# Kernelized attention and two expert layers on one core: the attention's TensorE work of a pair issued as one chunk

## The chip, the cores and the metric

The kernel runs on one core of one Trainium2 chip. The metric is the device time of one execution in microseconds; the kernel before takes 1374.68 us (median of three runs, 1373.49 to 1375.31).

## The reference

Three layers follow one another. Only the first is touched by the change.

```
proj = x @ w_phi                      # 64 -> 128 features, for q and for k, per head
proj = proj - max(abs(proj))          # over the 128 features of a token
phi  = concat(exp(proj), exp(-proj))  # 256 features
kv   = k_p.T @ v;  z = sum(k_p)       # over the 576 tokens
out  = (q_p @ kv) / (q_p . z + 1e-6)
# then x @ w_in, ELU, @ w_out         # 2304 x 512 -> 2048 -> 512
# then 4 experts: relu(x @ w1[e]) @ w2[e], weighted by normalized probabilities
```

There are 4 batches of 8 heads with 576 tokens and 64 channels; two heads make a pair, so there are 16 pairs, four to a batch.

## The kernel before

Attention goes pair by pair. The generator `attention()` (line 340 on) is a three-deep pipeline. In round `i` it holds the new pair `new` (number `i`), the pair `a` (`i-1`) and the pair `z` (`i-2`). Of `new` it makes the projections: `mid()` for the tokens left over from whole blocks of 128 (L229), `keys()` and `queries()` (both L237). After each projection VectorE applies the guard (L211 a maximum, L212 a subtraction), and ScalarE the exponentials of the keys (L215, L216). Of `a` it makes `kv()` (L266, L267; the PSUM bank is copied to `kvw` at L270), the transposes of the guarded queries `qd` (L277, L281, followed by exponentials into `ew`, L286), the denominators `den()` (L295) and the numerators `num()` (L308). `den()` also sends the denominators through a DMA (`dn<-dd`, L299), which lays them out on 128 partitions. Of `z` it makes three steps that need no TensorE: `rec()` (L314, L315 on VectorE, then the DMA L316 to DRAM), `spread()` (two DMAs L321, which read the reciprocals back over all partitions into `rb`), and `put_x()` (L327 on VectorE, then the two halves `xh` and `xl` of the attention's output on ScalarE, L333, and GpSimd, L336).

```
def rec(self):
    with tc.issue_after(mark[0]):
        V.tensor_scalar(out=dn, in0=dn, scalar1=1e-6, ...)
        V.reciprocal(out=dn, in_=dn)
    SP.dma_start(rscr[self.i]..., dn)
def spread(self):
    for h in range(2):
        SP.dma_start(self.rb[h * D:h * D + D], rscr[self.i]...)
def put_x(self):
    with tc.issue_after(mark[0]):
        V.tensor_tensor(out=xf, in0=xf, in1=self.rb, op=ALU.mult)
```

`mark[0]` is the last guard or Elu instruction issued on VectorE, so `rec()` and `put_x()` come behind it there. `dn`, `dd` and `rb` have one buffer each, `nd` has two. A `yield True` ends a chunk, a `yield False` does not.

The first four pairs are run ahead of everything else (the prologue). Then the second layer, `Elu`, begins. It is cut into 36 units, each of 24 matmuls in `l1` (L545 to L547) and 24 in `l2` (L575 to L577), with four calls of `slot()`. Each call adds `rate[0]` to a quota and, for each whole one, runs the attention to its next `yield True`. `RHEAD` is the rate for the first two token tiles, `RATE` for the next four. A limit (`limit[0]`) holds the attention at most one batch ahead of the need. Elu's matmuls are ordered behind the attention's last matmul (`pmark`). Its first tile needs `xh` and `xl` of the pairs 0 to 3, one pair for each quarter of its contraction (`kc`). PSUM has seven banks in this part of the kernel for `bank()`; Elu's accumulators take two and its current product one. Weight conversions (L119 to L155) run beside all this on ScalarE, VectorE and GpSimd. The scheduler may change the order of instructions of one engine that do not depend on each other. From about 430 us on there is no attention and no Elu, only the two expert layers (L673 to L777).

## Time and profile before

| | |
|---|---|
| median of three runs | 1374.68 us |
| profiled execution | 1376.91 us, of it span 1374.9 us |
| TensorE busy | 1344.1 us, 98% of the span |
| VectorE, ScalarE, GpSimd busy | 656.0, 594.4, 352.3 us |

TensorE is busy for nearly all of the span. The span lacks some 2 us of the execution's own time, which lie before its first and after its last instruction. L12 means line 12 of the kernel before; a matmul on 32-bit data appears as two instructions, so L237, 16 matmuls for a pair, shows as x32.

### The profile page before, as it was taken

The page shows a single profiled execution, that of the slowest core. Times are in us where ns is not written, and L with a number is a line of the kernel's source. Part 1 is how long each engine was busy: PE and PEld are TensorE (multiplying, and loading weights), DVE is VectorE, ACT ScalarE, POOL GpSimd, SP SyncE. Part 2 cuts the span into 40 slices and gives each one's busy share as a digit, 9 for nine tenths or more (in the row PEclk, how much of TensorE's full clock was granted, in tenths as well). Part 3 has the DMA queues.
Part 4 walks back from the last instruction along what each step waited for, and adds up shares of the span by engine and source line. Part 5 has one row for each costly group of instructions (what it writes and reads, how often), then busy time and mean ns, then how long its engine had stood idle before and what let it go on. Part 6 is the DMA issues. An engine that isn't in the chain of part 4 may idle for free.

```text
span 1374.9 us, 21612 instructions
## 1 busy us (share of the span) xinstructions
PE 1344.1 (98%) x8408; PEld 1220.7 (89%) x8408; DVE 656.0 (48%) x1085; ACT 594.4 (43%) x1268; POOL 352.3 (26%) x353
## 2 busy tenths in 40 slices
PE   8889999999999999989999999999999999999998
PEld 6688989898998999989888888889898988889897
DVE  5687556664754756674342433333432333423232
ACT  5687555555566554654333351213331213422121
POOL 2478333223463111264110350001420003500000
PEclk9999999999999999999999999999999999999999
DMA  7733344434423313364322045261354341542511
GB/s 226 220 90 98 110 122 151 119 123 124 132 85 108 104 47 115 108 240 170 145 103 116 31 161 182 81 212 46 106 193 161 102 151 32 161 161 92 196 58 62
DMA packets 98422, 173.43 MB, mean 126 GB/s; under 512 B 32272, under 2 KB 45712, under 8 KB 98320
## 3 DMA queue, kind: packets, MB, share of 16 engines
q1 hardware_dynamic: 83392, 148.25, 32.7%
q10 hardware_dynamic: 14928, 23.80, 5.5%
q8 instruction: 66, 1.08, 0.3%
q14 instruction: 36, 0.29, 0.1%
HBM read 118.13 MB, written 53.81 MB: 125 GB/s over the span
## 4 chain that ended last, share of the span: by engine, by line
PE 65%; DMA 4%; DVE 3%; issue 2%; ACT 2%; POOL 1%; SPq 0%; ACTq 0%; DVEq 0%; POOLq 0%
PE bank L673 10%; PE bank L675 9%; PE bank L674 9%; PE bank L775 9%; PE bank L776 9%; PE bank L777 9%; PE bank L754 2%; PE bank L753 2%; PE bank L752 2%; DMA yscr<-y 1%; DMA y<-yscr 1%; PE bank L576 0%; DVE y L785 0%; PE bank L577 0%; PE bank L575 0%
## 5 line engine op out<-in xcount | busy, mean ns | idle before, releaser
L673 PE MATMUL bank<-xv,w 128*128 128x384 f32 x840 | 280.1, 337 | 4.5 <-DVE h L690 1.7
L674 PE MATMUL bank<-xv,w 128*128 128x384 f32 x840 | 281.6, 335 | 0.0
L675 PE MATMUL bank<-xv,w 128*128 128x384 f32 x840 | 278.7, 336 | 0.0
L775 PE MATMUL bank<-w,h 128*128 128x512 f32 x576 | 225.7, 398 | 2.0 <-ACT h L689 1.8
L776 PE MATMUL bank<-w,h 128*128 128x512 f32 x576 | 227.3, 395 | 0.0
L777 PE MATMUL bank<-w,h 128*128 128x512 f32 x576 | 203.8, 396 | 0.0
L502 POOL TENSOR_TENSOR w<-wst,w 128x256 fp32r<-128x256 f32 x100 | 79.8, 815 | 412.8 <-ACT w L501 412.7
L673 PEld LDWEIGHTS bank<-xv,w 128*128 128x128 f32 x840 | 157.8, 188 | 14.2 <-DVE h L690 2.0
L674 PEld LDWEIGHTS bank<-xv,w 128*128 128x128 f32 x840 | 157.7, 188 | 5.3
L675 PEld LDWEIGHTS bank<-xv,w 128*128 128x128 f32 x840 | 157.4, 188 | 0.1
L689 ACT ACTIVATE h<-bank 128x384 fp32r<-128x384 f32 x144 | 67.8, 489 | 179.3 <-PE bank L675 105.0
L690 DVE SCALAR_TENSOR_TENSOR h<-bank,h 128x384 fp32r<-128x384 f32 x144 | 78.1, 555 | 138.2 <-ACT h L689 137.9
L775 PEld LDWEIGHTS bank<-w,h 128*128 128x128 f32 x576 | 107.7, 188 | 26.4 <-ACT h L689 4.0
L776 PEld LDWEIGHTS bank<-w,h 128*128 128x128 f32 x576 | 108.2, 188 | 22.8
L777 PEld LDWEIGHTS bank<-w,h 128*128 128x128 f32 x576 | 107.5, 188 | 22.0 <-DVE h L690 0.3
L679 ACT ACTIVATE cmab<-bank 128x384 f32<-128x384 f32 x60 | 29.4, 490 | 191.4 <-PE bank L675 191.4
L687 DVE TENSOR_TENSOR c<-cmab,bank 128x384 f32<-128x384 f32 x48 | 26.6, 554 | 133.1 <-ACT cmab L679 133.1
L545 PE MATMUL bank<-xh,w 128*128 128x256 f32 x288 | 82.7, 287 | 2.7 <-DVE kp L212 2.6
L624 POOL TENSOR_TENSOR xv<-xs,xv 128x768 fp32r<-128x768 f32 x24 | 46.6, 1944 | 147.1 <-ACT xv L623 141.6
L575 PE MATMUL bank<-gh,w 128*128 128x256 f32 x288 | 81.9, 285 | 0.0
L576 PE MATMUL bank<-gl,w 128*128 128x256 f32 x288 | 80.5, 280 | 0.3 <-DVE gl L558 0.3
L546 PE MATMUL bank<-xl,w 128*128 128x256 f32 x288 | 80.5, 280 | 0.2 <-POOL xl L336 0.2
(118 smaller groups left out, 2527.9 us busy)
## 6 DMA issues: line engine op xcount, KB each, us to landing
xv<-xvd SPq DMA_DIRECT2D x42, 768.0 KB, 4.6
wst<-in_w SPq DMA_DIRECT2D x64, 256.0 KB, 2.7
xvd<-xv SPq DMA_DIRECT2D x21, 768.0 KB, 5.3
yscr<-y SPq DMA_DIRECT2D x54, 256.0 KB, 3.7
y<-yscr ACTq DMA_DIRECT2D x54, 256.0 KB, 3.6
kq<-in_kq SPq DMA_DIRECT2D x16, 320.0 KB, 3.0
rb<-rec SPq DMA_DIRECT2D x32, 144.0 KB, 3.2
xscr<-nd ACTq DMA_DIRECT2D x16, 288.0 KB, 3.3
```

The lines of the kernel that those rows point to most:

```text
L502: on[WL[v % len(WL)]].tensor_tensor(out=lo, in0=x, in1=f32(hi), op=ALU.subtract)
L545: PE.matmul(ph[:, j], w[:, 0, c], xh[:, kc], start=(kc == j == 0), stop=False)
L546: PE.matmul(ph[:, j], w[:, 0, c], xl[:, kc], start=False, stop=False)
L575: PE.matmul(o, w[:, 0, c], self.gh[:, j], start=start, stop=False)
L576: PE.matmul(o, w[:, 0, c], self.gl[:, j], start=False, stop=False)
L673: PE.matmul(o, hi[:, c], x[:, 0, kc], start=not more and kc == 0, stop=False, skip_group_check=more)
L674: PE.matmul(o, hi[:, c], x[:, 1, kc], start=False, stop=False, skip_group_check=more)
L675: PE.matmul(o, lo[:, c], x[:, 0, kc], start=False, stop=kc == 1, skip_group_check=more)
L690: mark[0] = V.scalar_tensor_tensor(out=h[:, 1], in0=c, scalar=0.0, in1=f32(h[:, 0]), op0=ALU.max, op1=ALU.subtract).ins
L775: PE.matmul(self.acc, h[:, 0, c], w[:, 0], start=f == 0, stop=False)
L776: PE.matmul(self.acc, h[:, 0, c], w[:, 1], start=False, stop=False)
L777: PE.matmul(self.acc, h[:, 1, c], w[:, 0], start=False, stop=f == 2 * NQ - 1)
```

## The change

In each round the keys and queries of the new pair follow its middle projection at once, and no chunk ends between them. The steps of the pair `z` come after, each as a chunk of its own: reciprocals, spreading, and `put_x()`, which ends a chunk only where no pair `a` remains. There are three chunks to a round before and after. The two rates are raised by a third.

```
--- before.py
+++ after.py
@@ -42,8 +42,8 @@
 LAG = 2
 RING = 16
 PRE = 0.7
-RATE = 0.375
-RHEAD = 0.525
+RATE = 0.5
+RHEAD = 0.7
 WRATE = 3
 WHEAD = 3
 CVB = 3
@@ -345,9 +345,6 @@
             if a:
                 a.kv(0)
                 yield False
-            if z:
-                z.rec()
-            if a:
                 a.tpose(0)
                 a.kv(1)
                 yield False
@@ -355,27 +352,25 @@
                 a.tpose(2)
             if new:
                 new.mid()
-            if a or new:
-                yield True
-            if z:
-                z.spread()
-                yield True
-            if new:
                 keys = new.keys()
                 next(keys)
                 yield False
                 next(keys, None)
                 yield False
-            if z:
-                z.put_x()
-                done[0] += 1
-                yield not new
-            if new:
                 qs = new.queries()
                 next(qs)
                 yield False
                 next(qs, None)
+            if a or new:
                 yield True
+            if z:
+                z.rec()
+                yield True
+                z.spread()
+                yield True
+                z.put_x()
+                done[0] += 1
+                yield not a
             if a:
                 a.den()
                 yield False
```

The order on VectorE in the prologue, while pair 2 (its keys are `kp_478` here) is guarded; `dn`, `nd` and `rb` belong to pair 0, `raw`, `pcs` and `top` to the conversions. Before:

```order
L314 TENSOR_SCALAR dn<-dn 128x9
L124 TENSOR_SCALAR pcs<-pcs 128x512
L315 RECIPROCAL dn<-dn 128x9
L211 TENSOR_REDUCE mx<-bank 128x2
L212 TENSOR_TENSOR md<-bank,mx 128x256
L127 SCALAR_TENSOR_TENSOR top<-raw,pcs 128x512
L211 TENSOR_REDUCE mx<-bank 128x4
L128 TENSOR_SCALAR raw<-top 128x512
L211 TENSOR_REDUCE mx<-bank 128x4
L212 TENSOR_TENSOR kp_478<-bank,mx 128x4x128
L212 TENSOR_TENSOR kp_479<-bank,mx 128x4x128
L327 TENSOR_TENSOR nd<-nd,rb 128x576
```

The same place on VectorE after the change, from the guards of pair 2's queries (`qd_487`, `qd_488`) on:

```order
L212 TENSOR_TENSOR qd_487<-bank,mx 128x512
L212 TENSOR_TENSOR qd_488<-bank,mx 128x512
L127 SCALAR_TENSOR_TENSOR top<-raw,pcs 128x512
L314 TENSOR_SCALAR dn<-dn 128x9
L128 TENSOR_SCALAR raw<-top 128x512
L315 RECIPROCAL dn<-dn 128x9
L123 TENSOR_SCALAR pcs<-pcs 128x512
L124 TENSOR_SCALAR pcs<-pcs 128x512
L211 TENSOR_REDUCE mx<-bank 128x2
L212 TENSOR_TENSOR md<-bank,mx 128x256
L211 TENSOR_REDUCE mx<-bank 128x4
L327 TENSOR_TENSOR nd<-nd,rb 128x576
```

The reciprocal has moved from ahead of pair 2's guards to behind them, and the product with `rb` from ahead of pair 2's queries to the next pair's keys.

The second place is VectorE where Elu begins: before, from the reciprocal of pair 2 over the guards of pair 4 (`kp_795`):

```order
L314 TENSOR_SCALAR dn<-dn 128x9
L315 RECIPROCAL dn<-dn 128x9
L211 TENSOR_REDUCE mx<-bank 128x2
L212 TENSOR_TENSOR md<-bank,mx 128x256
L211 TENSOR_REDUCE mx<-bank 128x4 x2
L212 TENSOR_TENSOR kp_795<-bank,mx 128x4x128
L123 TENSOR_SCALAR pcs<-pcs 128x512
L212 TENSOR_TENSOR kp_796<-bank,mx 128x4x128
L327 TENSOR_TENSOR nd<-nd,rb 128x576
```

After the change, from the last guard of pair 4 (`qd_809`) to the first of pair 5 (`md`), with pair 2's reciprocal and product:

```order
L212 TENSOR_TENSOR qd_809<-bank,mx 128x512
L314 TENSOR_SCALAR dn<-dn 128x9
L123 TENSOR_SCALAR pcs<-pcs 128x512
L315 RECIPROCAL dn<-dn 128x9
L124 TENSOR_SCALAR pcs<-pcs 128x512
L127 SCALAR_TENSOR_TENSOR top<-raw,pcs 128x512
L128 TENSOR_SCALAR raw<-top 128x512
L327 TENSOR_TENSOR nd<-nd,rb 128x576
L211 TENSOR_REDUCE mx<-bank 128x2
L212 TENSOR_TENSOR md<-bank,mx 128x256
```

Between reciprocal and product stand pair 4's guards before, and only conversions after; the guards of pair 5 stand behind the product. The same order repeats for pair 3 behind pair 5's guards.

The third place is TensorE in the Elu stage, behind a pair's last transposes (`md`). Before:

```order
L281 MATMUL bank<-ident,md 128x128 x2
L229 MATMUL bank<-wbd,kq 128x256
L575 MATMUL bank<-gh,w 128x256
L576 MATMUL bank<-gl,w 128x256
L545 MATMUL bank<-xh,w 128x256
```

After, with Elu's lines five numbers lower:

```order
L281 MATMUL bank<-ident,md 128x128 x2
L229 MATMUL bank<-wbd,kq 128x256
L237 MATMUL bank<-wbd,kq 128x128 x16
L570 MATMUL bank<-gh,w 128x256
L571 MATMUL bank<-gl,w 128x256
```

The sixteen projections of keys and queries now follow the middle projection directly; before, Elu's matmuls stood in between. From the last attention matmul to the kernel's end the order on TensorE (5411 matmuls) is the same in both.

## Rows read from the trace of the kernel before

**Rows 1.** Stages: length, busy us of PE, PEld, DVE, ACT, POOL, granted clock, DMA.

```profile
20.00:73.00 53.00, 45.19 (x440) 35.85 (x440) 37.55 (x72) 36.63 (x84) 21.02 (x23) 1.00 0.65 199
...
73.00:125.00 52.00, 48.29 (x455) 43.32 (x456) 43.83 (x72) 41.92 (x90) 42.61 (x39) 1.00 0.26 77
...
125.00:325.00 200.00, 199.87 (x1841) 180.20 (x1841) 118.12 (x204) 120.99 (x262) 66.94 (x68) 1.00 0.42 127
...
325.00:450.00 125.00, 121.75 (x934) 118.31 (x933) 73.62 (x104) 73.10 (x148) 54.75 (x53) 1.00 0.36 111
...
1371.00:1375.00 4.00, 0.00 (x0) 0.00 (x0) 0.75 (x1) 0.00 (x0) 0.00 (x0) 0.70 0.35 131
```

**Rows 2.** TensorE's waits from 0 to 125 us: total, times, longest.

```profile
PE bank L277 <- DVE qd L212: 6.1, 3, 2.6
...
PE bank L545 <- DVE kp L212: 2.6, 1, 2.6
...
PE bank L308 <- DVE qd L212: 1.2, 1, 1.2
```

**Rows 3.** TensorE in order of time (start, length): one period without a wait.

```profile
17.73 0.60 PE L229 MATMUL bank<-wbd,kq 128*128 128x256 f32 x2
...
18.26 2.06 PE L237 MATMUL bank<-wbd,kq 64*128 64x128 f32 x32
...
20.24 1.18 PE L295 MATMUL bank<-ew,kvw 128*32 128x288 f32 x16
...
21.35 2.16 PE L308 MATMUL bank<-ew,kvw 128*64 128x288 f32 x16
...
23.44 1.16 PE L266 MATMUL bank<-vt,kp 128*128 128x128 f32 x8
...
29.10 0.60 PE L229 MATMUL bank<-wbd,kq 128*128 128x256 f32 x2
```

**Rows 4.** TensorE in order of time: the later periods up to Elu's first matmuls.

```profile
57.99 0.60 PE L229 MATMUL bank<-wbd,kq 128*128 128x256 f32 x2
...
69.90 0.30 PE L277 MATMUL bank<-ident,qd 128*128 128x128 f32 x1 [2.64 <-DVE qd L212]
...
72.36 0.60 PE L229 MATMUL bank<-wbd,kq 128*128 128x256 f32 x2
...
81.98 1.10 PE L266 MATMUL bank<-vt,kp 128*128 128x128 f32 x8
```

**Rows 5.** VectorE in order of time: undisturbed guards, then the fourth period's waits.

```profile
19.45 1.29 DVE L211 TENSOR_REDUCE mx<-bank 128x4 f32<-128x512 f32 x2
...
60.12 0.17 DVE L314 TENSOR_SCALAR dn<-dn 128x9 f32<-128x9 f32 x1 [3.08 <-DMA dn<-dd]
...
66.59 0.76 DVE L327 TENSOR_TENSOR nd<-nd,rb 128x576 f32<-128x576 f32 x1 [2.26 <-DMA rb<-rec]
```

**Rows 6.** SyncE's queue in order of time, the fourth period.

```profile
60.57 0.34 SPq L316 DMA_DIRECT2D rec<-dn  x1
...
62.74 1.10 SPq L321 DMA_DIRECT2D rb<-rec  x2
```

**Rows 7.** ScalarE's queue and ScalarE in order of time, around Elu's start.

```profile
53.53 0.55 ACTq L299 DMA_DIRECT2D dn<-dd  x1
...
79.11 0.42 ACT L333 ACTIVATE xh<-nd 128x256 fp32r<-128x256 f32 x1 [0.18 <-DVE nd L327]
```

**Rows 8.** ScalarE in order of time: one pair in the Elu stage.

```profile
294.70 0.60 ACT L270 ACTIVATE kvw<-bank 128x512 f32<-128x512 f32 x1 [1.15 <-PE bank L267]
...
295.19 1.42 ACT L286 ACTIVATE ew<-bank 128x512 f32<-128x512 f32 x4
```

**Rows 9.** TensorE in order of time: the same pair's projections.

```profile
295.16 0.60 PE L229 MATMUL bank<-wbd,kq 128*128 128x256 f32 x2
...
302.75 2.06 PE L237 MATMUL bank<-wbd,kq 64*128 64x128 f32 x32
```

**Rows 10.** TensorE in order of time: the first pair's projections.

```profile
5.53 3.79 PE L237 MATMUL bank<-wbd,kq 64*128 64x128 f32 x32
```

More of the change, by code (lines that the diff above doesn't have):

```diff
@@ L44 @@
 PRE = 0.7
-RATE = 0.375
-RHEAD = 0.525
+RATE = 0.5
+RHEAD = 0.7
 WRATE = 3
@@ L347, in attention @@
                 yield False
-            if z:
-                z.rec()
-            if a:
                 a.tpose(0)
@@ L357, in attention @@
                 new.mid()
-            if a or new:
-                yield True
-            if z:
-                z.spread()
-                yield True
-            if new:
                 keys = new.keys()
@@ L368, in attention @@
                 yield False
-            if z:
-                z.put_x()
-                done[0] += 1
-                yield not new
-            if new:
                 qs = new.queries()
@@ L377, in attention @@
                 next(qs, None)
+            if a or new:
                 yield True
+            if z:
+                z.rec()
+                yield True
+                z.spread()
+                yield True
+                z.put_x()
+                done[0] += 1
+                yield not a
             if a:
```

## The prediction

> **What bounds the kernel now.** I read the stages first, then TensorE's waits, then each engine in order of time. The stages show TensorE busy in 199.87 of 200 us between 125 and 325 us [rows 1]. There it is the bound, and a change of order gives nothing back. It is short of work earlier: 45.19 of 53 us in the prologue (20 to 73 us) and 48.29 of 52 us where Elu begins (73 to 125 us). The list of waits names the cause [rows 2]: transposes (L277) waited 6.1 us for guarded queries `qd`, and two waits behind Elu's start took 2.6 and 1.2 us. All end with VectorE, but VectorE is not full in the prologue (37.55 of 53 us).
>
> Why it is late stands on VectorE itself [rows 5]. In the fourth period `rec()` (L314) stood 3.08 us until the denominators' DMA had landed, and `put_x()` (L327) stood 2.26 us until `rb` had. Both are ahead of the new pair's guards in that engine's queue, so two DMA waits of an old pair hold up the new one. The DMA in question was issued by ScalarE's queue at 53.53 and ended the wait at 60.12, 6.6 us [rows 5, 7]; from the issue of the reciprocals (60.57) to `rb` (66.59) are 6.0 us, of them 2.2 until the second step's issue (62.74) [rows 5, 6].
>
> A period without such waits is the second: from L229 at 17.73 to L229 at 29.10, 11.37 us [rows 3]. The next three periods end at 72.36 [rows 4].
>
> **The change part by part.** No matmul, guard or transfer is added or removed, and TensorE's order behind the attention is the same, so whatever TensorE gains or loses before some 325 us passes to the end.
>
> *Prologue.* Three periods take 72.36 - 29.10 = 43.26 us; without waits 3 x 11.37 = 34.11. So 9.15 us can be had. In the new order the reciprocal comes behind the pair's own guards. Four guards with 512 elements cost eight operations of 0.6 us (two reductions in 1.29 us, pipelined [rows 5]), 4.8 us. The first starts 19.45 - 17.73 = 1.7 us into the period, so the queries are guarded after 6.5 us, with two conversion operations of the same kind after 7.7. The transposes are wanted 23.44 - 17.73 = 5.7 us plus the first half of `kv()` (some 2.3 of the 5.66 us up to 29.10), 8.0 us into it [rows 3]. That fits. By then the denominators have had more than 6.6 us. The product with `rb` now stands among the next pair's keys guards; `rb` lands 6.0 us after the reciprocal, some 3 us into the next period, which costs VectorE 1 to 2 us where its margin is 0.3. I leave 0.7 us of waiting over the three periods: **-8.4 us** (bounds -9.15 and -6).
>
> *Where Elu begins.* Here the change adds a wait. Take 0 at the start of pair 5's middle projection. Pair 2's reciprocal follows pair 4's guards and is ready about 2.4 us before 0 (the 7.7 us above, `put_x()` of pair 1 with its wait, and the reciprocal among conversions make 9.2 of 11.6 us). `rb` lands 6.0 us later, at 3.6. Until then VectorE stands at `put_x()`, and pair 5's guards are queued behind it. Product 0.7, the middle guard 0.8, eight guards and two conversions 6.0: the queries are guarded at 11.1, pair 3's reciprocal is ready at 12.0, its `rb` lands at 18.0. Then the product (0.7), `xh` on ScalarE (0.42 [rows 7]) and `xl` on GpSimd (about as long as the product, 0.7) follow, 19.8, and Elu's six matmuls on pair 3, which end at 20.5. TensorE reaches this point earlier: in the kernel before, the projections of pair 5, Elu's first unit and the sums of pair 4 took 81.98 - 72.36 = 9.62 us [rows 4]. To these come sums and transposes of pair 5 (29.10 - 23.44 = 5.66 [rows 3]) and half of pair 6's projections (1.5), less three matmuls, 16.4 us. So 20.5 - 16.4: **+4.1 us**, bounds 1.3 (`rb` a microsecond faster twice, and no wait at the first) and 6.2.
>
> The granted clock is 1.00 in every stage with matmuls, waits of 2.64 us included, and 0.70 in 1371 to 1375 us, where none runs [rows 1, 4]. [...]
>
> *The two later waits.* The 2.6 and 1.2 us behind Elu's start [rows 2] came from bringing a pair's keys and queries late, right ahead of work that wants their banks. Now 24 to 48 Elu matmuls follow the queries and give the guards time. But conversions still fill VectorE there (43.83 of 52 us [rows 1]). I take 3.8 away and put 1.5 back: **-2.3 us** (bounds -3.8 and +1.2).
>
> *Ten bursts.* For the pairs 6 to 15 all of a pair's projections follow its transposes without Elu between. Seven banks, less three for Elu, leave four, so the third and fourth projection bank are those that ScalarE must first empty. In a pair before, it copied `kvw` at 294.70 and ended the last exponentials at 295.19 + 1.42 = 296.61, 1.45 us after L229 began at 295.16 [rows 8, 9]. The projections came only at 302.75, so this cost nothing. In the new order the third bank is wanted after 0.53 + 0.99 = 1.5 us (L229, then half of L237's 1.98 [rows 3]) and the fourth after 2.0. That is just in time if ScalarE does nothing else first, and one conversion between (0.6) costs up to half a microsecond. From below the cost is 0, from above 1.2 us for each burst (two operations of 0.6); I take 0.2, nearer to the row, where the end was in time: **+2 us** (bounds 0 and 12).
>
> The higher rates move work within the stage: twelve pairs need 36 chunks either way, and the limit holds them back. VectorE has room after 125 us (118.12 of 200). Nothing, then.
>
> The sum: -8.4 + 4.1 - 2.3 + 2.0 = -4.6 us. It is made against the profiled execution (span 1374.9 in 1376.91 us), which is 2.2 us above the median; the difference is taken from the median: 1374.68 - 4.6 = 1370.1 us.
>
> **The rivals.**
> 1. *Elu's start takes the gain back.* The wait for pair 3's `xh` is at its upper end (6.2) and the two later waits come again elsewhere (0 instead of -2.3): -8.4 + 6.2 + 0 + 2.0 = -0.2, 1374.5 us. For it: VectorE and GpSimd are nearly full from 73 to 125 us. Against it: pair 5's work covers a part.
> 2. *Slower: the burst runs out of banks.* ScalarE is behind by two operations at each of ten bursts, 1.2 us each: -8.4 + 4.1 - 2.3 + 12 = +5.4, 1380.1 us. It outweighs the gain from 0.66 us for each burst on. For it: ScalarE has a queue in order, and `xh`, which waits for `rb`, now stands ahead of the burst. Against it: the row in which the exponentials end just in time, and ScalarE's 120.99 busy of 200 us.
> 3. *The clock falls in the new wait.* The first block of L237 in the kernel, when TensorE had just begun, took 3.79 us, the second 2.06 [rows 3, 10]. One such block more (+1.7) and half as much again behind it give +2.6: -2.0, 1372.7 us. The row's granted clock reads 1.00 at the start too, so the price is uncertain.
> 4. *All waits go.* The entry costs its lower bound and the bursts nothing: -8.4 + 1.3 - 2.3 = -9.4, 1365.3 us.
> That the change does little is excluded for the prologue: TensorE's order hardly moves there, but VectorE's does, and that is the engine waited for.
>
> **How the numbers follow.** Forecast 0.47, rival 1 0.20, rival 2 0.12, rival 3 0.08, rival 4 0.13. Less than 0.2% (2.75 us) can't be told from no change in this kernel. Faster: forecast, rival 4 and the better part of a quarter of rival 3, 0.62. Same: rival 1 and most of rival 3, 0.26. Slower: 0.12. The range 1365.8 to 1376.5 leaves out most of rival 2 and the best of rival 4. The forecast's own range is 1368 to 1372.
>
> **What would show it.** In the changed profile the starts of L229 in the prologue should be 11.4 to 12 us apart, pair 5's at about 64 us instead of 72.36. L314 should wait for no DMA in the prologue, and L327 for 3 to 5 us ahead of pair 5's guards. TensorE should show one wait of 3 to 5 us for `xh` or `xl` at some 80 us, and from 125 us on less than 4 us without work. I am wrong if L277 still waits for `qd` for microseconds, if the wait at Elu's start is above 6 us, or if waits at the projections (L237) for ScalarE recur with every pair.

## The result: 20 us slower, and the profile after

The changed kernel takes 1394.78 us (median of 4 runs, 1393.25 to 1397.62), the kernel before 1374.99 us (4 runs, 1373.49 to 1376.38) beside it on the same chip. The ratio is 1.0144, its 95% interval 1.0132 to 1.0157. The forecast was 1370.1 us, the range 1365.8 to 1376.5: wrong in sign.

To see where the time went I give each point of Elu a *loss*: its time less the undisturbed time of all TensorE work that is ordered ahead of it (0.53 us for a pair's L229, 1.98 for its L237 and so on, 11.3 us a pair, close to the 11.37 us period of [rows 3]; 0.118 us for each Elu matmul, as their starts lie apart in the trace). Two kernels that do the same work in another order can be compared by their losses, not by their times. u0, u6, u24 and u35 are the starts of the numbered Elu units, the end of Elu is the first L668 (L673 before), the rest is from there to the end of the span.

```
us lost             to u0   u0-u6   u6-u24   u24-u35   u35-end   sum at end of Elu   rest of span
before              19.4     5.4      3.3       1.4       0.0          29.4             961.5
changed             19.4     8.6      6.7       6.9       4.1          45.6             962.8
```

Five places, then: the prologue gained nothing, Elu's first units lost 3.2 us more than before, the middle 3.4, Elu's last units 5.5, the step to the expert layers 4.1, and the expert layers 1.3. They add to the 17.5 us between the spans 1374.9 and 1392.4; the medians lie 19.8 us apart, since the profiled execution of the kernel before was one of its slower ones.

Lines below 340 have the same number in both kernels, later ones are 5 lower in the changed kernel. The stages of the changed kernel answer to [rows 1] (length, busy us of PE, PEld, DVE, ACT, POOL, granted clock, DMA):

```profile
20.00:73.00 53.00, 48.03 (x416) 37.85 (x412) 34.98 (x63) 35.57 (x80) 20.01 (x20) 0.94 0.61 191
73.00:125.00 52.00, 50.80 (x467) 42.88 (x467) 43.57 (x73) 40.68 (x92) 32.59 (x33) 1.00 0.30 88
125.00:325.00 200.00, 198.38 (x1781) 178.82 (x1781) 113.36 (x200) 122.61 (x256) 73.20 (x75) 1.00 0.38 117
325.00:450.00 125.00, 114.13 (x889) 111.83 (x886) 66.65 (x91) 63.30 (x127) 50.49 (x49) 0.97 0.35 110
```

TensorE is busier in the prologue than before (48.03 against 45.19 us), at a granted clock of 0.94: busy, but partly at half speed (0.50 from 55 to 60 us). From 325 to 450 us it is busy for 7.6 us less. In the kernel before the granted clock is 1.00 throughout, up to the last matmuls.

**The prologue.** Pair 3's L229 in the kernel before:

```profile
42.95 0.60 PE L229 MATMUL bank<-wbd,kq 128*128 128x256 f32 x2
```

TensorE in order of time in the changed kernel (start, length, in brackets the idle time before and what ended it) answers to [rows 4]:

```profile
38.73 0.60 PE L229 MATMUL bank<-wbd,kq 128*128 128x256 f32 x2
...
55.15 0.80 PE L266 MATMUL bank<-vt,kp 128*128 128x128 f32 x2 [4.06 <-ACT kp L216]
59.36 1.06 PE L229 MATMUL bank<-wbd,kq 128*128 128x256 f32 x2
72.47 0.60 PE L229 MATMUL bank<-wbd,kq 128*128 128x256 f32 x2
```

Pair 3's L229 came at 38.73, 4.2 us ahead of the kernel before. Then one period took 20.63 us, and pair 5's L229 starts at 72.47, as before (72.36). The wait that did it is for keys' exponentials on ScalarE. ScalarE and its queue in the same stretch:

```profile
45.42 0.36 ACTq L335 DMA_DIRECT2D xscr<-nd  x1
...
54.17 0.41 ACT L309 ACTIVATE nd<-bank 128x288 f32<-128x288 f32 x1 [5.74 <-DMA xscr<-nd]
54.47 0.62 ACT L216 ACTIVATE kp<-kp 128x512 f32<-128x512 f32 x1
```

`num()` copies a pair's numerators into `nd` (L309). `nd` has two buffers, and the one it wants is that of the pair two rounds earlier, which `put_x()` sends to DRAM (L335). Before the change `put_x()` stood between the new pair's keys and queries; now it stands behind both. In the kernel before the DMA of pair 0 was issued at 37.70, 16.7 us ahead of the copy of pair 2 that wants the buffer (L309 at 54.38). In the changed kernel it is issued at 45.42, and ended the wait 8.7 us later. ScalarE stood 5.74 us at L309, and the exponentials queued behind it held TensorE for 4.06 us. The granted clock followed:

```profile
50.00:55.00 5.00, 1.08 (x10) 0.89 (x9) 0.58 (x2) 0.83 (x3) 1.71 (x2) 0.87 0.60 220
55.00:60.00 5.00, 4.85 (x21) 4.55 (x21) 3.19 (x5) 4.70 (x11) 2.25 (x2) 0.50 0.17 33
```

TensorE had worked 1.08 of 5 us; then the granted clock was 0.50, and L229 took 1.06 us in place of 0.60. The third rival named such a fall of the clock, at another place.

It happened three times in all. The granted clock also falls behind a wait at Elu's end and one at the step to the expert layers, both shown below:

```profile
364.30:367.70 3.40, 2.81 (x13) 2.82 (x14) 3.40 (x5) 2.09 (x4) 1.62 (x1) 0.50 0.51 181
429.00:433.00 4.00, 3.39 (x12) 3.39 (x13) 0.00 (x0) 1.56 (x3) 1.28 (x1) 0.57 0.65 214
```

An estimate of the price: in the three stretches at half speed (53.7 to 60.5, 364.3 to 367.7, 429.2 to 432.6 us) TensorE is busy for 5.4, 2.8 and 3.0 us; at the granted clocks of 0.50, 0.50 and 0.51 half of that, 5.6 us, is what full speed would have spared. L229 fits: from its start to that of L237 are 0.99 us at 59.36 and 0.53 in [rows 3].

**The middle.** The projections of the pairs 6 to 15 are the ten bursts. Nine of the ten start without a wait, one waits for ScalarE:

```profile
128.65 3.17 PE L237 MATMUL bank<-wbd,kq 64*128 64x128 f32 x32 [1.62 <-ACT ew L286]
```

**Elu's last units.** VectorE in order of time, first in the kernel before, then in the changed kernel:

```profile
344.98 0.70 DVE L128 TENSOR_SCALAR w<-top 128x512 uint32<-128x512 uint32 x1
...
353.29 0.96 DVE L630 TENSOR_TENSOR xt<-xs 128x768 f32<-128x768 f32 x1 [2.17 <-DMA xs<-xscr]
```

```profile
344.87 0.96 DVE L625 TENSOR_TENSOR xt<-xs 128x768 f32<-128x768 f32 x1 [1.69 <-DMA xs<-xscr]
...
348.27 0.68 DVE L127 SCALAR_TENSOR_TENSOR top<-w,pcs 128x512 uint32<-128x512 uint32 x1
348.87 1.46 DVE L619 TENSOR_TENSOR xv<-xt,xv 128x768 fp32r<-128x768 f32 x1
350.25 2.08 DVE L128 TENSOR_SCALAR w<-top 128x512 uint32<-128x512 uint32 x1
...
362.64 0.42 DVE L128 TENSOR_SCALAR w<-top 128x512 uint32<-128x512 uint32 x1
...
363.31 1.52 DVE L553 TENSOR_TENSOR gl<-g,gh 128x512 fp32r<-128x512 f32 x1
```

L625 and L619 are `split_x()`, which prepares the input of the expert layers; L123 to L128 are the weight conversions, L551 and L553 Elu's gates. In the kernel before the first L630 (the same line) starts at 353.29, when VectorE's last conversion step, at 344.98, is over. In the changed kernel it starts at 344.87, among the last conversions, and Elu's `gl` comes late. Measured from the start of u24 (338.4 before, 345.0 changed) that is 14.9 us behind it before and at its very start now. The last conversion's L124 moved the other way, from 5.1 us behind u24 to 12.9. GpSimd at the same time, and TensorE's wait:

```profile
347.65 4.39 POOL L619 TENSOR_TENSOR xv<-xs,xv 128x768 fp32r<-128x768 f32 x2 [5.02 <-ACT xv L618]
...
364.36 1.62 POOL L132 TENSOR_TENSOR top<-top,w 128x512 f32<-128x512 f32 x1
```

```profile
362.23 0.39 PE L570 MATMUL bank<-gh,w 128*128 128x256 f32 x1 [1.73 <-ACT gh L552]
364.88 0.58 PE L571 MATMUL bank<-gl,w 128*128 128x256 f32 x1 [2.27 <-DVE gl L553]
```

The same L128 takes 0.42 us at 362.64, when GpSimd is idle, and 2.08 us at 350.25, when two L619 on GpSimd fill 347.65 to 352.04. Of the 32 L128 of the changed kernel the eight that run beside a GpSimd instruction for 0.2 us or more take 0.46 to 2.08 us, the others 0.42 to 0.44. No run here takes GpSimd's part away, so the cause is not shown.

**The step to the expert layers.** ScalarE's last copy of Elu's sums, and TensorE's first matmul of the next stage:

```profile
428.96 0.60 ACT L588 ACTIVATE xs<-bank 128x512 f32<-128x512 f32 x1 [1.54 <-DMA x1scr<-xs]
```

```profile
429.61 0.69 PE L668 MATMUL bank<-xv,w 128*128 128x384 f32 x1 [3.96 <-ACT xs L588]
```

In the kernel before TensorE went on at once there.

### The profile page after: what moved, and what is told of

Same layout as the page of the kernel before. It is cut to its first block, busy times and chain, and to the rows that moved or that the text cites. A ratio compares the mean times of both kernels' runs of the same rounds, so it can differ in the third digit from the quotient of the medians.

```text
span 1392.4 us, 21608 instructions
## 1 busy us (share of the span) xinstructions
PE 1357.7 (98%) x8408; PEld 1230.2 (88%) x8408; DVE 655.9 (47%) x1085; ACT 597.3 (43%) x1268; POOL 352.2 (25%) x353
## 3 DMA queue, kind: packets, MB, share of 16 engines
q8 instruction: 66, 1.08, 0.3%
## 4 chain that ended last, share of the span: by engine, by line
PE 82%; DMA 8%; DVE 5%; ACT 2%; issue 2%; POOL 1%; SPq 0%; ACTq 0%; DVEq 0%; POOLq 0%
PE bank L668 10%; PE bank L670 9%; PE bank L669 9%; PE bank L770 9%; PE bank L771 9%; PE bank L772 9%; PE bank L266 3%; PE bank L237 2%; PE bank L540 2%; PE bank L749 2%; PE bank L747 2%; PE bank L748 2%; PE bank L541 2%; PE bank L542 2%; PE bank L570 2%
## 5 line engine op out<-in xcount | busy, mean ns | idle before, releaser
L668 PE MATMUL bank<-xv,w 128*128 128x384 f32 x840 | 280.7, 337 | 7.3 <-ACT xs L588 4.0
L669 PE MATMUL bank<-xv,w 128*128 128x384 f32 x840 | 282.1, 336 | 0.0
L668 PEld LDWEIGHTS bank<-xv,w 128*128 128x128 f32 x840 | 158.3, 188 | 17.3 <-ACT xs L588 4.2
L669 PEld LDWEIGHTS bank<-xv,w 128*128 128x128 f32 x840 | 158.2, 188 | 5.3
L619 POOL TENSOR_TENSOR xv<-xs,xv 128x768 fp32r<-128x768 f32 x24 | 46.9, 1955 | 142.3 <-ACT xv L618 136.8
L540 PE MATMUL bank<-xh,w 128*128 128x256 f32 x288 | 81.2, 282 | 0.6 <-ACT xh L333 0.6
```

The lines of the kernel that those rows point to most:

```text
L540: PE.matmul(ph[:, j], w[:, 0, c], xh[:, kc], start=(kc == j == 0), stop=False)
L668: PE.matmul(o, hi[:, c], x[:, 0, kc], start=not more and kc == 0, stop=False, skip_group_check=more)
L669: PE.matmul(o, hi[:, c], x[:, 1, kc], start=False, stop=False, skip_group_check=more)
```

## The experiments

Beside each kernel stands its ratio to the kernel before, in the text with the 95% interval; the changed kernel's is 1.0144. The losses come from one profiled execution each, and executions of one kernel differ by 4 to 10 us, so a loss is read for its place and the ratio for its size. The last column but one is the rest of the span, 961.5 us before and 962.8 in the changed kernel. nd3 is three buffers of `nd`, gp the product with `rb` on GpSimd.

```
us lost                     ratio    to u0   u0-u6   u6-u24   u24-u35   u35-end    sum     rest     profiled run
e1  old rates               1.0048   18.7     7.5      5.6      -0.1       0.0     31.7    961.0    1378.69
e2  new rates, old order    1.0056   18.4     7.3      2.8       1.5       0.0     29.9    962.3    1378.00
e3  nd3                     1.0100   15.0     7.6      6.3       6.0       4.0     38.9    961.6    1386.23
e4  early conversions       1.0054   16.0     7.8      6.3       3.0       0.0     33.2    960.9    1380.09
e5  WSLOW 1.6               1.0100   20.9    10.7      7.1       0.3       4.4     43.3    963.7    1392.98
e6  chunk cut               1.0060   17.7    13.6      6.6       0.9       0.0     38.8    961.4    1385.97
e7  chunk cut, nd3          1.0030   14.6    10.3      5.9       1.1       0.0     31.9    962.3    1379.99
e8  old rates, nd3          1.0014   14.9    11.7      6.1      -0.1       0.0     32.5    963.3    1381.81
e9  split_x late            1.0150   20.3    10.0      6.0      -0.1       7.6     43.7    969.1    1398.69
e10 pcs in the first bank   1.0080   16.4     9.4      6.0       7.4       0.0     39.3    958.8    1383.88
e11 nd3, e9, e10            1.0072   14.8     8.2      6.0      -0.1       2.7     31.5    964.2    1381.55
e12 another order, nd3      1.0028   15.1     7.7      5.2       0.3       2.0     30.3    964.8    1380.87
e13 nd3, gp                 1.0036   13.4     4.8      6.0       8.5       0.0     32.7    958.4    1376.84
e14 old rates, nd3, gp, e10 1.0019   15.7     6.6      6.1       0.5       0.0     28.9    966.1    1380.75
e15 before, gp              1.0117   22.8    12.3      9.0       5.3       0.0     49.4    959.8    1395.02
e16 e12, gp, e10            1.0045   14.3     9.5      5.2       7.8       0.0     36.8    961.6    1384.27
e17 e13, e10, RATE 0.375    0.9998   13.9     5.4      3.6       3.9       0.0     26.8    960.6    1373.14
e18 e13, e10, WSLOW 1.5     1.0008   14.7     5.2      6.7       2.6       0.0     29.1    960.5    1375.34
```

**The rates and the order apart.** e1 is the changed kernel with

```
-RATE = 0.5
-RHEAD = 0.7
+RATE = 0.375
+RHEAD = 0.525
```

> The new order of a pair's steps, with the two rates of the kernel before (0.375 and 0.525 steps for each Elu unit). Theory A (the order itself costs: the prologue gains nothing, the bursts cost some 7 us, conversions that come late cost some 10 us where Elu ends): within 3 us of the changed kernel, 1391 to 1397 us. Rival R (the higher rates cost: pairs follow each other too closely between 80 and 345 us and push the conversions back): at least half of the 20 us comes back, 1385 us or less.

Measured 1381.48 us, 1.0048 (1.0033 to 1.0063). Two thirds of the loss is gone, so theory A fell as it stood and rival R held. It went at Elu's end (7.0 us of it in the profile), at the step to the expert layers (4.1) and, with 1 us or so each, in the other columns. The first L625 starts at 351.54 in place of 344.87, 9.3 us behind the start of u24, and TensorE is busy throughout. The row of that stretch in e1:

```profile
345.00:370.00 25.00, 25.00 (x215) 25.00 (x214) 22.16 (x26) 13.33 (x21) 13.64 (x9) 1.00 0.54 161
```

e2 gives the kernel before the two new rates.

> The order of the kernel before, with the new rates (0.5 and 0.7). Theory A: within 3 us of the kernel before, 1372 to 1378 us. Rival R: 1385 us or more.

Measured 1381.67 us (10 runs, 1377.13 to 1387.55), 1.0056 (1.0037 to 1.0074): between the two. The rates cost the old order some 7 us as well. The profiled execution, at 1378.00, shows 0.5 us of them at the end of Elu and 0.7 behind it; where the other executions lose more was not profiled and stays open. In that profile `split_x()` starts early too, 5.7 us behind u24, but the last L128 is at 345.40, beside its first step, and u24 to u35 lose only 1.5 us.

**The prologue's wait.** e3:

```
-self.nd = a1.tile([P, S], F32, tag="nd", name="nd", bufs=2)
+self.nd = a1.tile([P, S], F32, tag="nd", name="nd", bufs=3)
```

> The changed kernel with three buffers of nd in place of two, so that num's copy (L309) no longer waits until the DMA of the x of two pairs before has read its buffer. Theory A: L309's 5.74 us before 54.17 goes, and with it TensorE's 4.06 us at 55.15 and the lower clock of 40 to 60 us (0.84); the transition from prologue to Elu comes 4 to 8 us earlier. If TensorE's gain passes to the end: 1387 to 1391 us. Rival C (the conversions set what happens at Elu's end, and they do not come earlier): the gain is lost again by 369 us, 1392 to 1396 us. Rival N (the wait only moves to the next DMA in the chain, rb or dn): prologue within 1.5 us of the changed kernel.

Measured 1388.49 us, 1.0100 (1.0078 to 1.0122), as theory A has it. ScalarE's rows show the mechanism: no wait, and the exponentials at 48.23 in place of 54.47.

```profile
47.94 0.39 ACT L309 ACTIVATE nd<-bank 128x288 f32<-128x288 f32 x1
48.23 0.62 ACT L216 ACTIVATE kp<-kp 128x512 f32<-128x512 f32 x1
```

The granted clock is 1.00 from 40 to 60 us, and 4.4 us fewer are lost up to u0. So the wait was for the buffer. The same edit on top of the old rates (e8) and of the cut chunk (e7) gave 4.7 and 4.1 us by the ratios.

> The changed kernel with the old rates and three buffers of nd. If the parts add: 1381.5 - 6 = 1375.5, 1374 to 1377 us, with the bursts' loss of some 13 us from u0 to u24 still there. Rival C (the prologue's gain is lost again where the conversions end): 1380 us or more.

e8: 1377.15 us, 1.0014 (1.0000 to 1.0028), at the edge of the expectation and not to be told from the kernel before. Its profile shows what Elu's start can take back once the prologue is faster. TensorE in order of time, then two stretches:

```profile
85.54 0.39 PE L540 MATMUL bank<-xh,w 128*128 128x256 f32 x1 [1.43 <-ACT xh L333]
86.35 0.39 PE L541 MATMUL bank<-xl,w 128*128 128x256 f32 x1 [0.42 <-POOL xl L336]
```

```profile
80.00:90.00 10.00, 8.15 (x64) 7.20 (x62) 5.23 (x10) 6.50 (x17) 4.37 (x6) 0.85 0.33 91
90.00:100.00 10.00, 10.00 (x76) 8.59 (x76) 6.96 (x14) 6.99 (x14) 4.66 (x4) 0.81 0.30 89
```

That is the wait for pair 3's `xh` that the forecast put at Elu's start (1.85 us in place of 4.1) with the third rival's fall of the clock behind it. In the changed kernel it is shorter (0.65 and 0.42 us). Why is not shown: it does not simply follow the prologue, for e5, whose prologue loses more than the changed kernel's, waits 1.62 and 0.4 us there.

**Conversions and split_x at Elu's end.** Three edits. e4 runs the conversions of the prologue earlier (`PRE = 1.0` in place of 0.7), e5 those of Elu's middle tiles (`WSLOW = 1.6` in place of 1.3), and e9 leaves them and holds `split_x()` back:

```
 def sub(d, x, y):
-    V.tensor_tensor(out=d, in0=x, in1=y, op=ALU.subtract)
+    with behind(mark):
+        V.tensor_tensor(out=d, in0=x, in1=y, op=ALU.subtract)
```

> The changed kernel with one conversion step for each attention step of the prologue in place of 0.7, so that the conversions run earlier. Theory A (conversions that come late collide with split_x at Elu's end, some 10 us between 345 and 430 us): that part goes, the last L132 comes before 345 us, 1384 to 1388 us. Rival P (the prologue is VectorE's: each conversion more there lengthens it by its own 1.8 us on that engine): the prologue ends 5 us or more later and the time is 1394 us or more.

e4: 1382.30 us, 1.0054 (1.0031 to 1.0077). Better than expected, but not for the reason: its last L132 starts at 359.4, not before 345. Of the 12.4 us in the sums 3.4 lie in the prologue (L309 waits 2.96 us and the clock stays at 1.00), 3.9 at Elu's end and 4.1 in the step to the expert layers. A conversion's four steps on VectorE (L123, L124, L127, L128) take 2.5 us in the kernel before, not rival P's 1.8. The run tells little by itself.

> The changed kernel with 1.6 conversion steps for each slot of Elu's middle tiles in place of 1.3; the prologue is untouched. Theory A (conversions that come late collide with split_x on VectorE at Elu's end): the last L132 comes before 352 us in place of 364, and the losses from u24 to the end of Elu (7.0 us) and in the transition (4.1 us) mostly go: 1383 to 1388 us. Rival S (split_x and the gates alone fill VectorE there): that loss stays above 8 us, 1391 us or more. Rival D (conversions packed more densely take VectorE from the bursts): the loss up to u24 rises by 3 us or more, 1388 us or more although the end is clean.

e5: 1389.10 us, 1.0100 (1.0078 to 1.0123). Elu's end is clean (0.3 us lost, TensorE busy 25.00 of 25 us from 345 to 370), the step to the expert layers still loses 4.4. So the two are separate things, which theory A had as one. The signs that rival D named are there as well: 4.0 us more lost up to u24, and a time above 1388. But 3.6 of them lie before u6, where the edit changes nothing; from u6 to u24, where it acts, the loss rises by 0.4.

> The changed kernel with split_x's subtractions held behind the last gate that was written before them, so that on VectorE the first of them stands behind gate 30 with all 32 conversions done (in the changed kernel behind gate 23, among conversions 30 to 32; in the kernel before behind gate 26). Theory A2 (the pairs end earlier at the higher rates, split_x becomes ready earlier and is put among the last conversions and gates): the loss from u24 to u35, 6.9 us, falls below 2 us; the transition's 4.1 us stays: 1386 to 1390 us. Rival L (the conversions are late whatever split_x does): the loss stays above 5 us, 1393 us or more.

e9: 1396.11 us, 1.0150 (1.0120 to 1.0181). The first subtraction now starts at 379.81, and u24 to u35 lose nothing: the last conversion's L124 comes 6.2 us behind u24 again, where it came at 12.9. So it was `split_x()` that pushed the last conversions back, and rival L falls, though its range holds the time. Theory A2's place is right, its time is not: `split_x()` now runs beside Elu's very last gates, the step loses 7.6 us, and the rest of the span takes 6.3 us more. The edit holds back every later `split_x()` as well, and the next one keeps TensorE waiting in the expert layers (5.48 us), and the two L669 behind that wait take 1.01 us, where two such matmuls take 0.51 in e13 (422.55). TensorE's three waits:

```profile
420.14 0.39 PE L571 MATMUL bank<-gl,w 128*128 128x256 f32 x1 [1.46 <-DVE gl L553]
427.70 0.69 PE L669 MATMUL bank<-xv,w 128*128 128x384 f32 x1 [4.70 <-ACT xs L588]
...
620.99 1.01 PE L669 MATMUL bank<-xv,w 128*128 128x384 f32 x2 [5.48 <-ACT xv L618]
```

**The step to the expert layers.** e10 changes which PSUM bank is the next stage's first:

```
-psum = [pool("psum", 7, space=PSUM, stack=pst)]
 pcs = pool("pc", 1, space=PSUM, stack=pst).tile(...)
+psum = [pool("psum", 7, space=PSUM, stack=pst)]
```

> The changed kernel with the conversions' bank pcs given the first of the eight PSUM banks in place of the last, so that the first bank of the next stage is the conversions' and not one that Elu's last sums still fill. Theory K (TensorE's 3.96 us before 429.61 are a wait for the bank that the last copy of xs by ScalarE empties, a matter of which bank falls first): the wait falls below 1 us, 1389 to 1392 us. Rival G (the last unit's gate comes late there because conversions and weights are late, and the banks do not matter): the wait stays above 3 us, 1393 us or more.

e10: 1385.03 us, 1.0080 (1.0053 to 1.0107). The wait is gone (loss 0.0), as theory K has it; Elu's end loses 7.4 us as before. The time is lower than theory K said: 8.8 us by the ratios, where the wait (4.0) and the half-speed stretch behind it (1.5, the estimate above) make 5.5. The order of every engine is the same in both kernels, and the profile's other gains (3.0 us in the prologue, 4.0 in the rest of the span with the half-speed stretch) lie where the edit reorders nothing; the two intervals leave room for a spread between executions of that size. In e4, e6 and e7 no such wait comes by itself. In e1, e2 and e18 a shorter one (0.99, 1.72 and 1.13 us) comes 4 to 5 us later, and in e14, which has this edit, one of 3.56 us:

```profile
417.64 0.69 PE L667 MATMUL bank<-xv,w 128*128 128x384 f32 x1 [3.56 <-ACT xs L587]
```

So the 4 us are an accident of which bank comes round, and no cost of the order or the rates as such; the edit moves the wait and does not always remove it.

> The changed kernel, its order and rates kept, with three edits: three buffers of nd, split_x's subtractions behind the gate, pcs in the first bank. If the four losses are separate and add (prologue 6, Elu's end 6, transition 4 us): 1394.8 - 16 = 1378.8, 1376 to 1382 us, what is left over the kernel before being the bursts. Rival C (they share one cause, the late conversions, or what one gives another takes): 1384 us or more.

e11, all three edits: 1385.21 us, 1.0072 (1.0045 to 1.0099), where 1376 to 1382 was expected; rival C's range holds it. The fixes do not add: the late `split_x()` still costs 2.7 us at the step, and TensorE waits 5.49 us for the next one at 606.81, so that the rest of the span takes 964.2 us in place of 962.8.

**The bursts.** e6 puts Elu's matmuls between keys and queries again; e7 is e6 with nd3:

```
                 next(keys, None)
-                yield False
+                yield True
                 qs = new.queries()
```

> The changed kernel with the chunk of a pair cut in two, keys in one and queries in the next, with Elu's matmuls between (four chunks for each pair at 0.5 a unit: the pairs go at the pace of the experiment with the old rates). Theory B (a burst wants a third and fourth projection bank that ScalarE has not emptied yet, about 0.8 to 1.1 us for each pair): the loss from u0 to u24, 13.1 us with the old rates and 15.2 us in the changed kernel, falls to 8 to 10 us, as before; prologue as in the changed kernel; 1376 to 1379 us. Rival Q (the loss is due to the reciprocal, spreading and x as steps of their own behind the pair, not to the chunk): the loss stays at 12 to 14 us, 1380 to 1383 us.

> The cut chunk together with three buffers of nd. If the parts add (the prologue's 6 us from nd, the bursts' 4 us from the cut): 1370 to 1373 us, faster than the kernel before. Rival C (what is gained in front is lost again where the conversions end): 1376 us or more.

e6: 1383.78 us, 1.0060 (1.0039 to 1.0082); e7: 1380.34 us, 1.0030 (1.0015 to 1.0046). e6 misses both theories, and e7 lies in rival C's range without its sign (1.1 us lost where the conversions end). Up to u24 e6 loses 20.2 us from u0 on, not 8 to 10, most of it in the first six units (waits for `xh` of 0.66 and for `md` of 0.92 us, then 1.89 us at L237, clock 0.83 from 110 to 120 and 0.85 from 150 to 160). TensorE's projections in the changed kernel, then in e7,

```profile
199.17 0.60 PE L229 MATMUL bank<-wbd,kq 128*128 128x256 f32 x2
199.69 2.82 PE L237 MATMUL bank<-wbd,kq 64*128 64x128 f32 x32
```

```profile
246.14 0.60 PE L229 MATMUL bank<-wbd,kq 128*128 128x256 f32 x2
246.67 1.16 PE L237 MATMUL bank<-wbd,kq 64*128 64x128 f32 x16
250.78 1.16 PE L237 MATMUL bank<-wbd,kq 64*128 64x128 f32 x16
```

The whole block takes 2.6 to 2.9 us in most bursts, against 2.06 undisturbed [rows 9]: 0.55 to 0.85 us each, and 1.1 in the burst at 128.65. Cut in two, the keys' half takes 1.16 us in some pairs and 1.80 in others.

This is not a wait for a bank: the profile lists no idle time of TensorE in these blocks, and the same 2.60, 2.82 and 2.91 us come back in the changed kernel and in e1. What differs is the order inside the block, which the line x32 hides (two instructions to each of its 16 matmuls, on f32 words; Elu's matmuls, on fp32r words, show one each: L540 has 288). In the undisturbed block the matmuls of the pair's two heads, which read the partitions 0 to 63 and 64 to 127, alternate, and the trace starts them in twos, 7 ns apart (302.745 and 302.752). In the slow blocks the scheduler has put the four matmuls of one head ahead of the four of the other, and they start one by one, 0.11 us apart (from 220.50 on). In the programs as they are built (before, changed, e1, e7) the halves that run one head after the other are the slow ones, save where a wait is listed; a burst of e1 that alternates takes 2.19 us:

```profile
131.73 2.19 PE L237 MATMUL bank<-wbd,kq 64*128 64x128 f32 x32
```

Over the ten blocks of the changed kernel this makes 7.8 us, and the one wait of 1.62 us brings it to 9.4. Why the scheduler chose that order no run shows. In e6 only four of the ten pairs have slow halves; what that saves goes into the waits and the clock of 0.83 and 0.85 named above.

**VectorE's standing at the product.** e12 moves the DMA of the reciprocals under the queries (order: middle projection, a chunk's end, keys, reciprocal, a chunk's end, spreading, queries, a chunk's end, x; old rates; nd3).

> Another order, with three buffers of nd and the old rates: chunk one is x, sums, transposes and middle projection, chunk two keys and then the reciprocal, chunk three spreading and queries, and x behind the queries. No burst of all projections, and the 6 us of the spread's DMA lie under the queries' guards. Theory: prologue as with three buffers of nd (loss at u0 about 15 us in place of 19), no burst cost (u6 to u24 3 to 4 us in place of 6): 1368 to 1373 us. Rival E (Elu's start takes the prologue's gain back, by a wait for xh at its first unit and a fallen clock): loss from u0 to u6 above 9 us, 1374 to 1380 us.

e12: 1377.34 us, 1.0028 (1.0013 to 1.0043), in rival E's range though not by its loss (7.7 us from u0 to u6). Up to Elu's end it loses 0.9 us more than the kernel before, and 3.3 us in the rest of the span. Its VectorE still stands at the product, as in the kernel before (2.26 [rows 5]) and in the changed kernel. Changed kernel, then e12:

```profile
44.62 0.76 DVE L327 TENSOR_TENSOR nd<-nd,rb 128x576 f32<-128x576 f32 x1 [3.49 <-DMA rb<-rec]
...
74.07 0.76 DVE L327 TENSOR_TENSOR nd<-nd,rb 128x576 f32<-128x576 f32 x1 [3.39 <-DMA rb<-rec]
```

```profile
44.62 0.76 DVE L327 TENSOR_TENSOR nd<-nd,rb 128x576 f32<-128x576 f32 x1 [4.40 <-DMA rb<-rec]
```

The next pair's guards are queued behind it. So e13 to e16 take this product from VectorE:

```
-with tc.issue_after(mark[0]):
-    V.tensor_tensor(out=xf, in0=xf, in1=self.rb, op=ALU.mult)
+G.tensor_tensor(out=xf, in0=xf, in1=self.rb, op=ALU.mult)
```

> The changed kernel with three buffers of nd, and the product with rb taken from VectorE to GpSimd, so that VectorE no longer stands 3.3 to 4.4 us at L327 with the next pair's guards behind it. Theory W (that standing is what is left of the prologue's loss, and what makes Elu's start give back part of the gain): no guard waits behind a DMA, the loss at u0 falls from 15.0 us (three buffers alone) to 12 us or less, the one from u0 to u6 from 7.6 to 6 us or less: 1383 to 1386 us, against 1388.5 for three buffers alone. Rival H (rb lands when it lands, and TensorE wants xh of pair 3 no later than before, so the wait at Elu's start grows by what the prologue gains): loss at u6 as with three buffers alone, 22 to 24 us, 1387 to 1391 us.

e13 (changed kernel, nd3, gp): 1380.60 us, 1.0036 (1.0022 to 1.0051), 8.8 us below e3 by the ratios and lower than theory W said. Only a part of that is theory W's. In the profiles it gains 1.6 us up to u0 (13.4 lost, not 12 or less) and 2.8 from there to u6; Elu's end loses 2.5 more; and 4.0 us come back at the step to the expert layers, the accident of the banks, and 3.2 in the rest of the span. At u6 it has lost 18.2 us against 24.8 before. GpSimd stands in VectorE's place, where only conversions queue behind it:

```profile
58.97 1.41 POOL L326 TENSOR_TENSOR nd<-nd,rb 128x576 f32<-128x576 f32 x1 [4.53 <-DMA rb<-rec]
```

> Changed order, old rates, three buffers of nd, the product on GpSimd, pcs in the first bank. Theory W: the kernel with old rates and three buffers (1377.15 us) less 3 to 5 us: 1371 to 1374 us. Rival H: 1376 to 1379 us.

> The kernel before, with only the product with rb taken from VectorE to GpSimd. Theory W: of the 6.1 us that the transposes waited for qd before 73 us, those behind L327 (2.26 us a period) go, 1370 to 1373 us. Rival H (the reciprocal L314 stands as long at its own DMA, or Elu's start waits for xh instead): 1373.5 to 1376 us.

> The order with the reciprocal behind the keys and x behind the queries (1377.34 us, three buffers of nd, old rates), with the product on GpSimd and pcs in the first bank. Theory W: VectorE's 4.40 us before 44.62 and TensorE's 2.27 us at 47.89 go, the clock stays at full speed from 50 to 55 us (0.73 there), the transition's 1.85 us go: 1369 to 1373 us, faster than the kernel before. Rival H: 1375 us or more.

e14: 1377.91 us, 1.0019 (1.0005 to 1.0034), and e16: 1381.13 us, 1.0045 (1.0028 to 1.0061), miss theory W. e14 gains nothing on e8, which differs from it by the product and the bank (1.0014): its Elu start is better by 5.1 us, but the wait of 3.56 us at 417.64 follows, behind which L667 to L669 take 0.52 us each, in place of 0.34 ahead of it, and the rest of the span takes 966.1 us. In e16 the waits that theory W named are gone, but `gl` keeps TensorE waiting 5.07 us at Elu's end (358.82). e15 (the kernel before with the product on GpSimd): 1393.48 us, 1.0117 (1.0090 to 1.0145), misses both by far. In the old order the reciprocal stands ahead of the guards, at its own DMA. GpSimd, VectorE and TensorE of e15 in one period:

```profile
36.60 1.40 POOL L326 TENSOR_TENSOR nd<-nd,rb 128x576 f32<-128x576 f32 x1 [5.77 <-DMA rb<-rec]
```

```profile
29.68 1.18 DVE L314 TENSOR_SCALAR dn<-dn 128x9 f32<-128x9 f32 x1 [2.68 <-DMA dn<-dd]
```

```profile
39.60 2.08 PE L266 MATMUL bank<-vt,kp 128*128 128x128 f32 x8 [3.87 <-ACT kp L215]
```

The later product makes ScalarE wait 4.42 us at `xh`, with the keys' exponentials queued behind it. So the edit harms the old order. In the new order it paid with the new rates (e13 against e3) and not with the old ones (e14 against e8).

**Towards a faster kernel.** e17 and e18 are e13 with `pcs` in the first bank and one edit each for Elu's end: `RATE = 0.375`, or `WSLOW = 1.5`.

> The changed kernel with three buffers of nd, the product with rb on GpSimd, pcs in the first bank, and the old rate of 0.375 for Elu's middle tiles alone (0.7 stays for the first two). On VectorE split_x's first subtraction then stands behind gate 25 and all 32 conversions (23 and 30 with the new rate). If it is the middle rate that brings split_x among the conversions: the loss from u24 to u35, 8.5 us with the product on GpSimd alone, falls below 1 us, the loss at the end of Elu is 24 to 27 us (before 29.4): 1369 to 1372 us, faster than the kernel before. If some other thing (the conversions' own lateness) makes Elu's end slow: 1376 us or more.

> As the run before but with both new rates kept, and 1.5 in place of 1.3 conversion steps a slot in Elu's middle tiles: split_x's first subtraction stays early (gate 24) but has all 32 conversions ahead of it. If it is the conversions between split_x's steps that cost, and not split_x's early place: the loss from u24 to u35 falls below 1.5 us as well, 1370 to 1373 us. If split_x's early place alone costs: the loss there stays above 4 us, 1375 us or more.

e17: 1373.86 us, 0.9998 (0.9980 to 1.0015); e18: 1376.13 us, 1.0008 (0.9991 to 1.0025). Neither can be told from the kernel before. Each shrinks the 8.5 us of e13 at Elu's end, to 3.9 and 2.6 us, and neither to what was expected. What stands there now differs: in e18 still `gl` on VectorE (1.79 us before 353.72), in e17 the last pairs' `xh`, which the lower rate brings late:

```profile
337.56 0.38 PE L539 MATMUL bank<-xh,w 128*128 128x256 f32 x1 [2.06 <-ACT xh L332]
```

Both the middle rate and the conversions' own rate act on that place, so it is the meeting of `split_x()` and the last conversions that costs, not either alone; e2 and e9 say the same. No version is faster than the kernel before by more than its interval.

## Why the prediction was wrong

- **"Prologue -8.4" failed, and is 0.** The first half was right: up to 38.73 the periods were 11.4 us, and 4.2 us were gained. The step counted VectorE's queue and not ScalarE's: it moved `put_x()` later without asking what waits for `put_x()`'s own DMA. That DMA frees `nd`, and with two buffers ScalarE waits for it ahead of the keys' exponentials. e3 shows it: a third buffer gives 6 us back by the ratios. That pair 5's L229 came at 72.47, as before, is chance: a gain and a loss of the same size.
- **The product's wait** was foreseen (3 to 5 us at L327; 3.49 came in the prologue and 3.39 ahead of pair 5's guards) and priced at 1 to 2 us a period. Taking it from VectorE gave 4.4 us up to u6 in the profiles of e3 and e13, once `nd` was out of the way.
- **"Where Elu begins, +4.1"** was put at a wait for pair 3's `xh`. In the changed kernel that is 1.1 us in all; in e7 and e8 it is 1.9 to 2 us, in e8 with a granted clock of 0.85 and 0.81 behind it. The wait is there, the size was too large.
- **"The two later waits, -2.3"** was right in kind and too small: both are gone in the changed kernel, 3.8 us, the term's lower bound.
- **"Ten bursts, +2"** had the right place and neither the size nor the mechanism: the ten blocks cost 9.4 us, of them 1.62 the one wait for ScalarE that rival 2 named, and 7.8 the order of the two heads' matmuls. The prediction also let the fourth bank be wanted half a microsecond behind the third, while in the undisturbed block the two heads write their two banks side by side. The x16 in the order shown ahead of it hid the change inside the block. These three terms add to +6.7 us, against 6.6 lost between u0 and u24 (3.2 and 3.4).
- **"The higher rates ... Nothing, then"** failed. I counted room on VectorE between 125 and 325 us and did not follow what the earlier end of the pairs lets start: `split_x()` needs only the attention's output, so it moved forward into the last conversions and gates, in a stretch where VectorE was already busy 20.66 of 25 us before. On TensorE 108 more Elu matmuls stand behind the attention's last one than before, so the order that both kernels share covers the last 5410 matmuls and not all behind the attention. That cost 5.5 us at Elu's end, and it takes the new order and the new rates together: each alone (e2, e1) loses 1.5 us or less there. e5 and e9 each clear the place itself. The 13 us that e1 gives back by the rates are this, the 4.1 us of the banks and smaller parts.
- **"Whatever TensorE gains or loses before some 325 us passes to the end"** is right only as long as nothing waits there. Besides the 5.5 us at Elu's end, an unlucky bank cost 4.1 (e10) and the rest of the span 1.3. With the bursts and Elu's start this makes 17.6, for the 17.5 us between the spans.
- **The third rival** came true in kind: the granted clock fell to 0.50 or 0.51 at the waits for pair 3's keys (4.06 us), at Elu's end (1.73 and 2.27 us) and at the step (3.96 us), and not at Elu's start; by the estimate above it cost 5.6 of the 17.5 us, which lie inside the losses named.
- Open: what e2 loses in the executions that were not profiled, why u0 to u6 differs by up to 6 us between kernels that differ little there (e6 and e1), and why the rest of the span goes from 958 to 969 us where the waits named do not explain it.

## What to carry to other kernels

When a step is moved, list what waits for each of its outputs and for the DMA that frees its buffers, on every engine, before counting what it frees; a buffer count that suited the old place may not suit the new one. Work that finishes earlier lets its successors start earlier, and where they land is a term of the sum: look at the next crowded stretch, not only at the one that is changed. A loss seen in a profile may also be an accident of which bank or buffer comes round, and one edit that only renumbers them tells. A line that merges many matmuls hides their order: when a block takes longer and its engine does not idle, look at the order inside it.

## What was not expected of the hardware

The transfer `xscr<-nd` of 288 KB took 7.2 us in the median from issue to landing in the changed kernel and 3.3 us in the kernel before, by the profile's list of DMA issues, and 2.1 to 7.9 us in the other runs that list it; the one that held ScalarE ended the wait 8.7 us after its issue, and in its first part the DMA engines were 0.91 busy (45 to 50 us). What sets this time no run shows.

One VectorE instruction on 128x512 words (L128 of the changed kernel) took 0.42 us at 362.64, while GpSimd was idle, and 2.08 us at 350.25, while GpSimd worked beside it. What ties the two no run shows.

Sixteen projections, each on half of the partitions, took 2.06 us when the two halves alternated (302.75 in the kernel before) and 2.60 to 2.91 us in the changed kernel when four of one half stood ahead of four of the other, with TensorE busy all the time.

The granted clock stayed at 1.00 behind a wait of 2.64 us in the kernel before (69.90) and fell behind waits of 1.43 and 0.42 us in e8 (85.54 and 86.35; 0.85 and 0.81 in the stretches of 10 us around and behind them).
